# Pooled attention and four experts on one core: first batch in smaller pieces, chunk 0 in another order, batch 1 turned on TensorE

## The chip, the cores and the metric

One core of one Trainium2 chip runs the whole program in one launch. The metric is the device time of an execution in microseconds; the median of five is compared. The profiled execution also has a span, from its first to its last instruction, which is a little shorter.

## The reference

```python
# per batch (8), head (8): 576 queries of 64; keys and values are means of 8 rows
k_p = k.reshape(B, H, 72, 8, 64).mean(axis=3); v_p = ...
attn = softmax(q @ k_p.T / 8);  o = attn @ v_p
x = o.transpose(0, 2, 1, 3).reshape(4608, 512)
p = domain_probs / (domain_probs.sum(-1) + 1e-9)
out = sum over e of p[:, e] * (relu(x @ w1[e]) @ w2[e])   # w1: 512x1024, w2: 1024x512, 4 experts
```

All arrays are float32 in memory. Each expert works on every token, so two thirds and more of the arithmetic are the experts' matrix products.

## The kernel before, in words

**Chunks.** The tokens are worked in nine chunks of 512. Chunk c (0 to 7) holds the first 512 of the 576 queries of batch c; chunk 8 holds the last 64 queries of all eight batches ("remainder", `rem_*`). A chunk's hidden units lie as `H_sb` in four quarters: two halves of F by two halves of tokens.

**Attention of a batch** is a row of pieces, each a Python function that issues its instructions when it is called: the loads (`load_q`, and for keys and values `load_whole` for batches 0 and 1, or `load_part`, four parts that the DMA adds up, from batch 2 on); the pooling (`fold_keys`, `fold_values` on VectorE; for batch 0 `sum_keys`, `sum_values` as matmuls with the identity); `queries` and `keys`, which turn q and the pooled keys so that the head's dimension lies on partitions; `scores` with the exponential on ScalarE; `context`, a product with the pooled values and a column of eights, and a division on VectorE; `turn`, which brings the 128 x 512 token block into `xT`. For batch 0 `turn` uses TensorE with the identity and a copy out of PSUM; for all others a DMA transpose on the SP queue. `queries` and `keys` turn on TensorE for batches 0 and 1 (`BUSY = 2`) and by DMA from batch 2 on. All loads that cast or add go through GpSimd's queue (POOL), in program order with GpSimd's own additions.

**Experts.** In chunk 0, `up` is the plain first layer, one block of 128 hidden units at a time, with the relu on ScalarE; `down` is the second layer of expert 0 in seven products (a scheme of Strassen's kind, with the sums of weights `weight_sums` and of hidden units `hidden_sums` made on VectorE), `down_plain` that of experts 1 and 2. From chunk 1 on both layers are made of seven products instead of eight: `up_product` (with `first_weight_sums`, `x_sum`, and relus on ScalarE and VectorE, `relu_sum`) and `down`. In step 4 of `down` (`POOLED`) the addition to `acc` is GpSimd's, for experts 1 to 3.

**Order.** Everything stands under a manual schedule: the program order is the order of each engine. `attention_first` has batch 0's attention, with `idle(n)`, matmuls on zeros that fill TensorE's time and write nothing used, and then the first layer of expert 0 in token halves. Chunk 0 then runs in four rounds of eight steps, with a table (`pieces_first`) that puts batch 1's attention, weight sums and loads into steps. In the long loop, slot g = 7 t + i issues step i of expert t's first layer for two units and step i - 1 of the `down` of the expert before, thus 2 x 4 + 8 matmuls of 128x128x256. `pieces_later` puts batch b's pieces into slots counted from 28 (b - 2), 28 slots being one chunk:

```python
q_at, k_at, scores_at, contexts_at, loads_at = (
    (4, 10, (14, 15, 16, 17), (18, 19, 20, 22), (12, 14, 13, 16, 19)) if b == 2
    else (-4, -4, (3, 4, 5, 6), (8, 9, 11, 13), (-2, 17, 0, 3, 6)))
```

Here `loads_at` are the slots of the next batch's first part, its q, and its second to fourth part. A `turn` follows its context by one slot. The slot is a place in the program order; GpSimd or SP reach it when what stands before it on their own queue is done.

**Queues at the start.** SP: q of batch 0, in two halves. POOL: k and v of batch 0 in halves, `w1` of experts 0 and 1, the probabilities, `w2` of expert 0, `w1` of expert 2, batch 1's k, q, v, `w1` of expert 3, the other `w2`, the remainder's q, batch 2's first part. A piece `gate` (a small GpSimd copy from batch 1's `xT`) stands ahead of batch 2's second part.

Of the kernel before, what the change touches and what calls it, by code (L numbers as in the profile page):

```python
# [9 lines left out]
ACT = mybir.ActivationFunctionType  # L10
# [7 lines left out]
def kernel(  # L18
# [57 lines left out]
    gate_at = const.tile([1, NR], BF16, name="gate")  # L76
# [27 lines left out]
    def load_whole(b, src, nm):  # L104
# [4 lines left out]
        for hs in groups(b):  # L109
            nc.gpsimd.dma_start(  # L110
                out=raw[:, hs], in_=src[b, hs].rearrange("h (j r) d -> j h r d", r=POOL)
            )
# [10 lines left out]
    def load_q(b):  # L123
        q_sb = raws[("q", b)] = qpool.tile([P, H, NR, D], BF16, name="q_sb")
        src = q[b, :, 0:NT, :].rearrange("h (p r) d -> p h (r d)", r=NR)
        if b:
            nc.gpsimd.dma_start(out=q_sb[:].rearrange("p h r d -> p h (r d)"), in_=src)
            return

        wide = acc[:].rearrange("p r (g t) -> p (r g) t", t=NR * D)  # L130
        for hs in groups(b):
            nc.sync.dma_start(out=wide[:, hs], in_=src[:, hs])
        for pair in range(NPAIR):
# [110 lines left out]
    def sum_keys(hs):  # L244
        kp = sum_pool(raws[("kraw", 0)], hs)
        nc.vector.tensor_copy(out=kp_all[0:SP, hs, 0, :], in_=kp)
        nc.scalar.copy(out=kp_all[0:SP, hs, 1, :], in_=kp)
# [24 lines left out]
    def queries(b, pair=0):  # L272
# [9 lines left out]
        qt_ps = one_bank(b).bitcast(BF16)[:, 0:4 * P].rearrange("p (h a t) -> p h a t", h=2, a=2)  # L282
# [5 lines left out]
        nc.vector.tensor_copy(out=state[("qT", b)][:, 2 * pair:2 * pair + 2], in_=qt_ps)  # L288
# [49 lines left out]
    def turn(b, r):  # L338
# [4 lines left out]
        if b:  # L343
            nc.sync.dma_start_transpose(out=dst, in_=x_tok)
            return
        xt_ps = chains[0][:].bitcast(BF16)[:, 0:KC * P].rearrange("p (k t) -> p k t", t=P)
        for kc in range(KC):
            nc.tensor.transpose(xt_ps[:, kc, :], x_tok[:, kc * P:(kc + 1) * P], ident[:])
        nc.scalar.copy(out=dst, in_=xt_ps)
# [46 lines left out]

    def attention_first():

        lo, hi = groups(0)
        idle(24)  # L400
# [3 lines left out]
        idle(2)  # L404
        keys(0, lo)
        idle(2)
        sum_keys(hi)
        scores(0, 0)
        queries(0, 2)
        queries(0, 3)  # L410
        idle(1)
        scores(0, 1)
        keys(0, hi)
        sum_values(lo)
        scores(0, 2)
        sum_values(hi)
        idle(2)
        scores(0, 3)
        idle(6)
        half = NT // 2  # L420
        context(0, 0)
        context(0, 1)
        idle(3)
        turn(0, 0)
        context(0, 2)
        idle(2)
        turn(0, 1)
        context(0, 3)
        up(0, 0, range(0, 2), slice(0, half))
        turn(0, 2)  # L430
        up(0, 0, range(2, 4), slice(0, half))
        turn(0, 3)
        up(0, 0, range(4, FCH), slice(0, half))
        up(0, 0, range(FCH), slice(half, NT))
# [11 lines left out]
    def up(c, e, fcs, at=slice(0, NT)):  # L446
        xT, H_sb = x_of(c), hidden[(c, e)]
        for fc in fcs:
# [3 lines left out]
            for kc in range(KC):  # L452
# [6 lines left out]
                out=dst, in_=out_ps.rearrange("p (t n) -> p t n", n=HN), func=ACT.Relu)  # L459

# [162 lines left out]
    def down_last(c, e):  # L623
# [3 lines left out]
        for row in (1, 0):  # L627
            for col in range(2):
                cols = slice(col * HD, (col + 1) * HD)
                ps = banks[2 * row + col][:].rearrange("p (j d) -> p j d", j=BLOCKS)  # L630
                for j in range(BLOCKS):
                    for fc in range(FCH):
                        nc.tensor.matmul(  # L633
                            ps[:, j], lhsT=H_sb[:, fc // HF, row, fc % HF, j * P:(j + 1) * P],
                            rhs=last_weights(fc, col), start=(j == 0 and fc == 0),
                            stop=(fc == FCH - 1), skip_group_check=True,
                        )
                for j in range(BLOCKS):
                    add(ps[:, j], c, e, row * BLOCKS + j, cols, False)
# [34 lines left out]
    make_identity(nc, ident[:])  # L674
    every = slice(0, H)

    def gate():

        nc.gpsimd.tensor_copy(out=gate_at[:], in_=state[("xT", 1)][0:1, 0, 0:NT:P])

    def pieces_first():

        at = {}

        def put(s, i, *pieces):
            at.setdefault((s, i), []).extend(pieces)

        def put_each(slots, pieces):
            for slot, piece in zip(slots, pieces, strict=True):
                put(*slot, piece)  # L690

        put(0, 0, *weight_sums(0))
        put_each([(0, i) for i in range(3, 7)], first_weight_sums(0))
# [172 lines left out]
```

## Time and profile before

| | us |
|---|---|
| median of 5 runs (lowest, highest) | 506.93 (506.67, 508.61) |
| profiled execution, its own time | 506.93 |
| its span | 504.8 |
| TensorE busy (weight loads) | 493.8 (407.0) |
| VectorE, ScalarE, GpSimd busy | 377.9, 300.6, 119.4 |
| loaded and stored by DMA queues | 42.48 MB, mean 84 GB/s |

Busy times are sums over the span; TensorE's matmuls are pipelined and their ends are modelled, so what counts there is when the next one starts. In a timeline line the first two numbers are start and duration in us, then engine, line of the kernel, operation and tiles, the number of instructions merged, and in brackets the idle time before and what ended it. GpSimd's DMA instructions (L110 to L171) are issues: the transfer lands later, and the engine's wait before a later issue names the landing.

### The profile page before, as it was taken

The numbers are of one execution on the slowest core, as the hardware profiler recorded it, in microseconds if no ns is written. First come the engines' busy times: TensorE is split into PE (matmuls) and PEld (weight loads), VectorE is DVE, ScalarE is ACT, GpSimd is POOL, SyncE is SP. The second block draws the span as 40 slices with busy tenths as digits, with TensorE's granted clock in tenths as the row PEclk, the third lists the DMA queues.
The fourth block names the chain that finished last, engine by engine and source line by source line (L and its number), as shares of the span: only waits on it lengthen the run. The fifth ranks groups of instructions, "written<-read, shape, count | busy, mean of one in ns | idle before, by whom it ended". The sixth has DMA issues, their size and how long they took to land.

```text
span 504.8 us, 11277 instructions
## 1 busy us (share of the span) xinstructions
PE 493.8 (98%) x4580; PEld 407.0 (81%) x4580; DVE 377.9 (75%) x742; ACT 300.6 (60%) x558; POOL 119.4 (24%) x113
## 2 busy tenths in 40 slices
PE   9999999999999999999999999999999999999995
PEld 4657448878788887988788878888888888888885
DVE  3465689988867887788687868887787767876673
ACT  2675616685576557655766576656755566556650
POOL 6331033462560145112530244010001110111010
PEclk9999999999999999999999999999999999999998
DMA  9999969999699048922793179430310010003003
GB/s 187 209 206 208 201 70 127 151 93 119 67 127 123 8 50 118 126 55 34 66 163 64 26 74 159 47 56 22 84 34 1 22 64 1 12 21 84 1 1 84
DMA packets 106787, 42.48 MB, mean 84 GB/s; under 512 B 79840, under 2 KB 105184, under 8 KB 106736
## 3 DMA queue, kind: packets, MB, share of 16 engines
q0 software_dynamic: 59728, 22.43, 40.7%
q1 hardware_dynamic: 46432, 18.82, 19.3%
q8 instruction: 36, 0.59, 0.5%
q10 hardware_dynamic: 576, 0.52, 0.3%
q14 instruction: 15, 0.12, 0.1%
HBM read 45.69 MB, written 9.44 MB: 109 GB/s over the span
## 4 chain that ended last, share of the span: by engine, by line
PE 90%; DVE 5%; DMA 3%; ACT 1%; issue 1%; DVEq 0%; ACTq 0%
PE o_ps L578 37%; PE unit L510 35%; PE unit L453 5%; DMA xT<-x_tok 3%; PE o_ps L604 3%; PE unit L256 2%; PE att L304 2%; PE unit L633 1%; DVE S L187 1%; DVE acc L649 1%; PE att L330 1%; DVE H L491 1%; PE unit L240 1%; ACT o_ps L586 0%; DVE x_tok L319 0%
## 5 line engine op out<-in xcount | busy, mean ns | idle before, releaser
L649 DVE SCALAR_TENSOR_TENSOR acc<-o_ps,p_all,acc 128x256 f32<-128x256 f32 (+1 forms) x284 | 126.5, 486 | 57.3 <-PE o_ps L578 40.0
L578 PEld LDWEIGHTS <-H 128*128 128x128 bf16 x1320 | 129.1, 98 | 17.7 <-issue 1.6
L510 PEld LDWEIGHTS <-w_bf 128*128 128x128 bf16 x1024 | 98.0, 98 | 18.2 <-issue 6.5
L491 DVE CUSTOM_DVE_ANT_0 H<-unit,partial 128x512 bf16<-128x512 f32 x128 | 87.7, 686 | 23.2 <-PE unit L510 16.9
L578 PE MATMUL o_ps<-w_bf,H 128*128 128x256 bf16 x792 | 102.6, 273 | 0.7 <-ACT o_ps L586 0.6
L510 PE MATMUL unit<-xT,w_bf 128*128 128x256 bf16 x672 | 96.4, 273 | 1.0 <-ACT unit L523 0.7
L592 POOL TENSOR_TENSOR acc<-acc,addend 128x512 f32<-128x512 f32 x24 | 33.1, 1379 | 266.6 <-ACT addend L590 257.8
L525 ACT COPY partial<-unit 128x512 f32<-128x512 f32 x128 | 72.0, 590 | 31.4 <-PE unit L510 30.8
L510 PEld LDWEIGHTS <-wu_bf 128*128 128x128 bf16 x768 | 73.1, 98 | 10.8 <-issue 2.5
L510 PE MATMUL unit<-xs,wu_bf 128*128 128x256 bf16 x512 | 76.9, 273 | 0.0
L578 PE MATMUL o_ps<-wt_bf,H 128*128 128x256 bf16 x528 | 68.4, 273 | 0.0
L578 PEld LDWEIGHTS <-S 128*128 128x128 bf16 x528 | 51.7, 98 | 6.4
L523 ACT COPY unit<-unit 128x512 f32<-128x512 f32 x64 | 37.2, 582 | 31.9 <-PE unit L510 26.1
L527 ACT ACTIVATE H<-unit 128x512 bf16<-128x512 f32 x64 | 38.8, 606 | 27.6 <-PE unit L510 27.6
L531 ACT ACTIVATE H<-unit 128x512 bf16<-128x512 f32 x64 | 38.1, 596 | 27.7 <-PE unit L510 27.5
L510 PE MATMUL unit<-xs,w_bf 128*128 128x256 bf16 x256 | 38.5, 273 | 2.0 <-DVE H L491 2.0
L647 ACT ACTIVATE acc<-o_ps,p_all 128x256 f32<-128x256 f32 x72 | 30.2, 471 | 13.4 <-PE o_ps L578 10.8
L119 POOL DMA_DIRECT2D kraw<-in_k_dram x18 | 25.3, 1405 | 39.0 <-DMA kraw<-in_k_dram 38.8
L578 PE MATMUL o_ps<-w_bf,S 128*128 128x256 bf16 x264 | 34.2, 273 | 0.0
L578 PE MATMUL o_ps<-wt_bf,S 128*128 128x256 bf16 x264 | 34.2, 273 | 0.0
L510 PE MATMUL unit<-xT,wu_bf 128*128 128x256 bf16 x224 | 33.7, 273 | 0.0
L308 ACT ACTIVATE expT<-att 72x1024 bf16<-72x1024 f32 x28 | 28.6, 1020 | 7.8 <-PE att L304 7.8
(112 smaller groups left out, 525.6 us busy)
## 6 DMA issues: line engine op xcount, KB each, us to landing
out_dram<-acc SPq DMA_DIRECT2D x32, 256.0 KB, 3.3
w_bf<-in_moe_w_dram POOLq DMA_DIRECT2D x7, 1024.0 KB, 22.5
q_sb<-in_q_dram POOLq DMA_DIRECT2D x7, 512.0 KB, 10.6
kraw<-in_k_dram POOLq DMA_DIRECT2D x24, 144.0 KB, 5.6
vraw<-in_v_dram POOLq DMA_DIRECT2D x24, 144.0 KB, 6.6
acc<-in_q_dram SPq DMA_DIRECT2D x2, 512.0 KB, 4.6
w_bf<-in_moe_w_dram POOLq DMA_DIRECT2D x2, 512.0 KB, 11.6
wt_bf<-in_k_dram POOLq DMA_DIRECT2D x2, 288.0 KB, 7.7
```

The source lines that it names most:

```text
L119: nc.gpsimd.dma_start(out=raw[:], in_=rows, accum_op=ALU.add)
L308: nc.scalar.activation(out=expT[:, 2 * pair:2 * pair + 2].rearrange("j h a b t -> j b (h a) t"), in_=sc_ps[0:SP].rearrange("j b h (a t) -> ...
L491: nc.vector._custom_dve(TENSOR_ADD_SAT, out=dst, in0=ps, in1=part, s0=LARGEST, s1=0.0)
L510: nc.tensor.matmul(ps[:, n * HN:(n + 1) * HN], lhsT=lhs[:, kc, f:f + P], rhs=rhs[:, kc, :], start=(not grows and n == 0 and kc == 0), stop ...
L523: nc.scalar.copy(out=units[unit][1][:], in_=ps)
L525: nc.scalar.copy(out=part[:, step - 2], in_=ps)
L527: nc.scalar.activation(out=quarter(0, 0), in_=ps, func=ACT.Relu)
L531: nc.scalar.activation(out=quarter(0, 1), in_=ps, func=ACT.Relu)
L578: nc.tensor.matmul(ps[:, j], lhsT=lhs[:, i, j * P:(j + 1) * P], rhs=rhs[:, i, :], start=(not grows and i == 0 and j == 0), stop=(i == HF - 1),
L592: nc.gpsimd.tensor_add(out=dst, in0=dst, in1=addend[:])
L647: nc.scalar.activation(out=dst, in_=o_ps, func=ACT.Copy, scale=prob)
L649: nc.vector.scalar_tensor_tensor(out=dst, in0=o_ps, scalar=prob, in1=dst, op0=ALU.mult, op1=ALU.add,)
```

## The change

1. *Start.* q of batch 0 in halves by two ways: heads 0 to 3 on SP as before, heads 4 to 7 on POOL with the cast in the DMA, behind the two halves of k. The identity is made after the first k load is issued. `w1` of experts 2 and 3 are loaded ahead of batch 1's k, q and v.
2. *Batch 0's attention.* 16 fillers instead of 24 at the start, 20 in all instead of 42. `scores_first` works on four heads and half of the tokens, so that the exponentials of the first 256 tokens are there after two; `sum_keys` splits its copies by heads; the copies of `queries` and `turn` alternate between VectorE and ScalarE. `up_first` does the first layer of expert 0 for 128 tokens at a time (two quarters), two blocks of hidden units to a bank, between contexts and turns; tokens 256 to 511 follow by `up`.
3. *Chunk 0.* `first_chunk` is an order written out: expert 1's first layer; expert 2's with expert 0's `down`; expert 3's with batch 1's queries, keys and scores; then `down_plain` of experts 1 and 2 with batch 1's contexts and turns. Some weight sums go to slots of the long loop.
4. *Batch 1* is turned by TensorE (`turn`: `if b >= BUSY`), with the copy on ScalarE.
5. *Batch 2's loads.* No `gate`; the second and third part and q are issued before chunk 0, the fourth part in slot 3, ahead of GpSimd's first sum. Batches 2 and 3 get other slots.
6. *The end.* In `down_last` the last pair of sums has a bank for each.

```diff
+    def load_q(b, group=None): ...     # group 0: SP and cast copies; group 1 or none: POOL
@@ sum_keys
-        nc.vector.tensor_copy(out=kp_all[0:SP, hs, 0, :], in_=kp)
-        nc.scalar.copy(out=kp_all[0:SP, hs, 1, :], in_=kp)
+        n = (hs.stop - hs.start) // 2
+        for i, copy in enumerate((nc.vector.tensor_copy, nc.scalar.copy)):
+            part = slice(i * n, (i + 1) * n)
+            copy(out=kp_all[0:SP, hs][:, part],
+                 in_=kp[:, part].unsqueeze(2).to_broadcast([SP, n, 2, D]))
@@ turn
-        if b:
+        if b >= BUSY:
             nc.sync.dma_start_transpose(out=dst, in_=x_tok)
             return
@@ attention_first
+        idle(16)
+        sum_keys(lo)
+        queries(0, 0); queries(0, 1)
+        sum_keys(hi)
+        keys(0, lo)
+        queries(0, 2); queries(0, 3)
+        scores_first(0, 0)
+        keys(0, hi)
+        idle(2)
+        scores_first(1, 0); scores_first(0, 1)
+        sum_values(lo)
+        scores_first(1, 1)
+        sum_values(hi)
+        context(0, 0); context(0, 1)
+        idle(2)
+        turn(0, 0)
+        up_first(range(0, 4), first)
+        turn(0, 1)
+        context(0, 2)
+        up_first(range(4, FCH), first)
+        context(0, 3)
+        up_first(range(0, 4), second)
+        turn(0, 2)
+        up_first(range(4, 6), second)
+        turn(0, 3)
+        up_first(range(6, FCH), second)
+        up(0, 0, range(FCH), half)
+    def up_first(fcs, at):
+        for fc in fcs[::2]:
+            out_ps = (units[1] + chains[1:])[turn_of("up", 3)][:, 0:2 * P]
+            for i in range(2):
+                for kc in range(KC):
+                    nc.tensor.matmul(out_ps[:, i * P:(i + 1) * P],
+                        lhsT=w1_bf[:, 0, kc, (fc + i) * P:(fc + i + 1) * P], rhs=xT[:, kc, at], ...)
+            nc.scalar.activation(..., func=ACT.Relu)
@@ pieces_later
-                    (4, 10, (14, 15, 16, 17), (18, 19, 20, 22), (12, 14, 13, 16, 19)) if b == 2
+                    (1, 9, (13, 14, 15, 16), (17, 18, 20, 21), (11, 12, 14, 25, 28)) if b == 2
+                    else (0, 3, (10, 11, 12, 13), (15, 16, 18, 20), (5, 6, 8, 11, 14)) if b == 3
+            if b == 2:
+                put(start + 3, lambda: load_part(2, 3))
+                put(start + 5, lambda: load_q_rem(2))
...
-            for n, slot in enumerate((24, 25, 25, 26) if b == 2 else (16, 16, 20, 23) if b < B
+            for n, slot in enumerate((24, 25, 25, 26) if b == 2 else (24, 24, 25, 26) if b == 3
+                                     else (16, 16, 20, 23) if b < B
@@ the program
+        load_q(0, 0)
+        load_whole(0, k, "kraw", groups(0)[:1])
+        make_identity(nc, ident[:])
+        load_whole(0, k, "kraw", groups(0)[1:])
+        load_q(0, 1)
...
+        load_w1(2)
         load_w2(0)
-        load_w1(2)
+        load_w1(3)
         attention_first()
...
+        load_part(2, 0)
+        load_part(2, 1)
+        load_q(2)
+        load_part(2, 2)
         load_q_rem(0)
         load_q_rem(1)
-        load_part(2, 0)
+        first_chunk()
```

The remainder's pieces of batches 0 and 1 move from slots 0, 5, 9, 10 to 6, 10, 12, 13.

## The prediction

> **What bounds the kernel now.** I read the page's shares and slices first, then the busy time by stage, then the timeline of TensorE for gaps, and last the timelines of GpSimd, SyncE and VectorE around those gaps.
>
> ```profile
> span 504.8 us, 11277 instructions
> PE 493.8 (98%) x4580; PEld 407.0 (81%) x4580; DVE 377.9 (75%) x742; ACT 300.6 (60%) x558; POOL 119.4 (24%) x113
> ...
> DMA  9999969999699048922793179430310010003003
> GB/s 187 209 206 208 201 70 127 151 93 119 67 127 123 8 50 118 126 55 34 66 163 64 26 74 159 47 56 22 84 34 1 22 64 1 12 21 84 1 1 84
> ```
>
> TensorE is busy nearly everywhere, so only three things shorten the run: fewer matmul slots, an earlier start of useful ones, or fewer gaps. The DMA row is saturated for the first five slices (63 us, about 200 GB/s): until then the order of loads decides what is there.
>
> ```profile
> 0.00:22.24 22.24, 20.41 (x154) 11.05 (x155) 9.64 (x28) 8.30 (x11) 11.56 (x20) 1.00 1.08 198
> 22.24:30.32 8.08, 7.61 (x72) 6.71 (x72) 2.79 (x7) 6.80 (x18) 3.99 (x5) 1.00 1.21 207
> 30.32:73.73 43.41, 43.41 (x283) 22.90 (x283) 29.82 (x53) 21.57 (x37) 5.57 (x9) 1.00 1.14 173
> ...
> 124.20:131.20 7.00, 4.88 (x43) 3.92 (x41) 6.81 (x15) 2.38 (x5) 3.27 (x3) 1.00 0.45 83
> ```
>
> Stages (columns: length, then busy PE, PE weight load, DVE, ACT, POOL, clock, DMA share, GB/s): batch 0's attention and filler matmuls last to 22.24; its first layer for expert 0 to 30.32; the rest of chunk 0 to 73.73 without a gap. Then comes the long loop, in slots of 16 matmuls of 128x256 at 109 ns = 1.75 us. At 124 to 131 TensorE lacks 2.1 us, 2.4 with the slower matmuls beside it.
>
> ```profile
> 9.03 0.65 POOL L171 DMA_DIRECT2D p_all<-in_moe_domain_probs_dram  x1 [1.12 <-DMA wt_bf<-in_k_dram]
> 9.19 1.04 PE L240 MATMUL unit<-wt_bf,ident 72*72 72x256 bf16 x8
> 10.06 0.61 PE L285 MATMUL o_ps<-ident,q_sb 128*128 128x128 bf16 x8
> 10.51 0.59 PE L256 MATMUL unit<-H 128*128 128x512 bf16 x2
> ...
> 22.24 0.60 PE L453 MATMUL unit<-xT,w_bf 128*128 128x256 bf16 x4 [0.41 <-ACT xT L349]
> ```
>
> GpSimd's wait tells that the first half of k landed by 9.03; the fillers end at 9.19 and the key sums start. The first layer starts at 22.24, released by the copy of the second turned block.
>
> ```profile
> 115.13 1.40 POOL L119 DMA_DIRECT2D kraw<-in_k_dram  x1 [0.62 <-DMA kraw<-in_k_dram]
> 116.84 1.38 POOL L119 DMA_DIRECT2D vraw<-in_v_dram  x1 [0.31 <-DMA vraw<-in_v_dram]
> ...
> 124.39 0.43 DVE L187 TENSOR_TENSOR xs<-xT 128x512 bf16<-128x512 bf16 x1 [1.72 <-DMA xT<-x_tok]
> ...
> 126.13 0.60 PE L510 MATMUL unit<-xs,w_bf 128*128 128x256 bf16 x4 [0.89 <-DVE H L491]
> ...
> 129.59 0.60 PE L510 MATMUL unit<-xs,w_bf 128*128 128x256 bf16 x4 [1.11 <-DVE H L491]
> ```
>
> The gap's cause: batch 2's last DMA transposes (issued 116.02 and 119.45) share the engines with batch 3's last loads. VectorE, in order, waits 1.72 us for them, then also has batch 3's key and value sums (0.75 and 1.49 us) in hand, and TensorE waits for its relus.
>
> **The change, part by part**
>
> *Start.* Only half of q goes ahead on SP; the first k load goes ahead of the identity's memset on POOL. Both halves of q land by 6.56 (the casts start at 4.78 and 6.56), so the second takes about 1.8 us of a saturated system, and the issue moves from 1.37 to about 0.75. The first half of k then lands between 9.0 - 0.6 - 1.8 = 6.6 and 9.0 - 0.6 = 8.4; I take 7.3. The 16 fillers end near 7.5: the weight loads of before's stand 0.43 apart up to 6.7 us, 0.22 after. So key sums start near 7.5, 1.7 earlier.
>
> Then, by durations of before: key sums 0.87; VectorE and ScalarE copies start 1.07 after the sum and take 0.42 and 0.37. The second half of k lands 1.93 after the first (10.96 - 9.03), 9.2, so its sums run 9.2 to 10.1. The second half of q, now in POOL's queue, lands some 1.3 later (batch 1's whole q took 2.6: 37.2 to 39.8), 10.5. First scores at 11; four exponentials of 1.02 with the q copy ahead of them fill ScalarE to about 16. The second value sum ends at 15.3, and its copy at 15.9. Contexts start at 16.0 (before 18.6), the first division ends at 17.4, its turn's copy at 18.6 (before, context to end of copy: 18.60 to 21.13). The first layer by quarters needs just this one block: it starts at 18.6 instead of 22.24. From there 64 matmuls of 128 columns (3.6), 16 transposes and 2 contexts (1.4) and 32 of 256 columns (3.5) are 8.5. The two last turns share one bank with the copies (0.59, then 0.41), which I count as 0.4 of waits. Expert 1 starts at about 27.4 instead of 30.32: **-2.9** (-3.8 to -1.6).
>
> Here a rule of the Trainium skill speaks against the change: "TensorE: Matmul & The Clock Gate", section "Back-to-back issue gap", gives about 81 ns per matmul where each 128-column matmul has its own weight load. By it the 64 cost 5.2 us, 1.6 more. The row at 10.06 shows eight such pairs in 0.45 us (10.06 to 10.51), 56 ns. I take the row; by the rule the sum would be -1.4.
>
> *Batch 1 turned by TensorE.* Adds 16 transposes in a stage with no free slot and four ScalarE copies of 0.59 (ACT has 21.6 of 43.4 busy there, so those hide). Four transposes take 0.22 (42.66 to 42.88 in TensorE's timeline): **+0.9**. The same page's section on PE-mode transpose gives about 275 ns for one in a kernel: 4.4 us for 16, and a sum of +0.5 in all. Again the row decides, because these are the same shape and neighbours. It takes four DMA transposes (60.1 to 71.0) and GpSimd's gate off their queues; the gate waited 27.04 us for them.
>
> *Chunk 0's order.* The same matmuls. Loads: expert 2's first weights take the place of the second weights of expert 0 (29.4), these land at 34.6, expert 3's first weights at about 39.8, batch 1's k, q, v at 42.4, 45.0, 48.5, and expert 1's second weights at 54.2 as before (all from GpSimd's and VectorE's waits, shifted by 5.2 for one weight load). They are needed at 36.1 (bank opening on TensorE), 47.5, 48 to 55, and 56.6. Slack is 1.5, 8, 3 to 7, 2.4 us, so nothing waits if the loads keep their pace. For bank waits among queries and contexts (each waits for a 0.41 copy or 0.9 division behind it on VectorE, which loses eight weight sums of 0.6 to later slots or other places): **+0.4** (0 to 1.5). The loop starts at about 72.1.
>
> *Batch 2's loads ahead of the sums.* Its second part is no longer held by the gate to 72.0 but by the first part's landing, about 65. Before, from there to the issue of the last part's v is 16.3 us (72.03 to 88.32); so 81.5, and GpSimd's first sum (g = 5, ScalarE's addend ready near 82) comes at 83, a store behind it on SP at 84, the remainder's q transpose at 85, landing 2.4 to 4.4 later; its scores (slot 10) come at 91. **+0.2** (0 to 2).
>
> *Batch 2's attention a slot earlier, batch 3's folds moved from slots 24 and 25 to 31 and 32.* The last transpose is issued 1.75 to 2 us earlier relative to the loop. Batch 3's third part comes after GpSimd's sum of slot 19, thus still beside these transposes (4.4 to 7.7 us each). VectorE's need at 122.7 (before's clock) meets a landing between 121.8 and 125.1, and the folds are out of its way. Of the 2.4 us I take **-2.0** (-2.4 to -0.5).
>
> *New places.* Batch 3's last part follows GpSimd's sum of slot 26: issued 125.3 and 126.7, landing 5 to 6.6 later at 130.3 to 133.3, and its folds come at 131.8 and 133.6: **+0.4** (0 to 4). Batch 3's x sums (four of 0.42) now fall in slots 52 to 54 together with batch 4's folds (0.75 and 0.42 to 1.5): VectorE at about 80% in this stretch gets 3 us more in 5.25, so relus run late: **+0.7** (0 to 2). Its transposes at slots 44 to 49 leave the place at 160, where TensorE loses 0.5: **-0.3** (-0.6 to 0).
>
> *Tail.*
>
> ```profile
> 498.03 0.88 DVE L649 SCALAR_TENSOR_TENSOR acc<-unit,p_all,acc 128x256 f32<-128x256 f32 x2 [0.80 <-PE unit L633]
> ...
> 499.78 0.88 DVE L649 SCALAR_TENSOR_TENSOR acc<-unit,p_all,acc 128x256 f32<-128x256 f32 x2 [0.87 <-PE unit L633]
> ```
>
> The last pair of adds starts when both halves of a bank are done. With its own bank the first add runs beside the last eight matmuls: **-0.4**, with nothing behind it but the store.
>
> *Sum*: -2.9 + 0.9 + 0.4 + 0.2 - 2.0 + 0.4 + 0.7 - 0.3 - 0.4 = **-3.0**. The profiled execution took 506.93, its span 504.8 and 2.1 around it; that is also the median of the five runs. Forecast 503.9.
>
> **The rivals**
>
> *The loads hold it.* The first half of k lands at 8.4 rather than 7.3, with TensorE idle for it, and all after it in the queue likewise; and at slot 24 the transposes are as late as before. Front -1.8, boundary -0.5, no gain at 160: -1.8 + 0.9 + 0.4 + 0.2 - 0.5 + 0.4 + 0.7 - 0.4 = -0.1, 506.8. For it: DMA at 9 tenths in these slices. Against: 512 KB is really taken from ahead of k. Chance 0.16.
>
> *Slower: batch 3's last loads miss their fold.* At slot 31 VectorE, strictly in order, waits for k's last part; behind it stand relus that free TensorE's banks, and the 1.72 us wait before cost 2.4. With lateness d the loss is d + 0.7, in place of my 0.4: 503.5 + d + 0.7. The gain is gone at d = 2.7, and it is slower by 0.3% from d = 4.3; at 5 it is 509.2. It needs the sum of slot 26 to be held on GpSimd, as it was by 8.82 us for VectorE at 127.04. Against: that hold came of the gap which goes. Chance 0.14.
>
> *More than forecast.* The boundary's wait goes wholly, slot 52 costs nothing, the front gives 3.6: 0.4 + 0.7 + 0.7 more, 502.1. Chance 0.12. The main case has 0.58.
>
> **How the numbers follow.** 0.3% is 1.5 us, about what a measurement here can tell from none: faster is under 505.4, slower over 508.45. Main case and the better one lie under 505.4 together: 0.70. Same 0.16, slower 0.14. The likeliest cases alone span 501 to 505.5; to hold 8 in 10 the range takes in the first rival and half-late loads: 500.9 to 508.0.
>
> **What would show it.** Right: key sums near 7.5, first layer near 18.6 and at 56 ns per 128-column matmul, expert 1 near 27.4, the loop's start near 72, no VectorE wait for xT at slot 24, a last add of 0.49 alone. Wrong: key sums at 8.4 or later with TensorE idle ahead; the bank opening waiting for w2; scores of the remainder waiting for qTr; VectorE waiting for kraw or vraw at slots 31 and 32; gaps at slot 52 or after.

## The result, and the profile after

The changed kernel took 503.52 us (median of 40 runs), the kernel before 507.67 us (77 runs beside them): a ratio of 0.9914, 95% interval 0.9898 to 0.9931. By the ratio that is 4.4 us less (by the two medians 4.2), where 3.0 were forecast and 503.9 us were named. That the median lies so close to 503.9 is partly luck: the kernel before took 507.67 us here, not the 506.93 from which the forecast was counted. The ratios leave out disturbed executions, the medians do not.

The profiled execution took 502.04 us. Its page answers to the one of before:

```profile
span 500.3 us, 11351 instructions
PE 490.2 (98%) x4622; PEld 407.1 (81%) x4622; DVE 372.9 (75%) x741; ACT 302.4 (60%) x561; POOL 119.5 (24%) x113
...
DMA  9999999989499759923894179740210010004003
GB/s 161 212 210 203 203 84 129 131 66 100 59 136 66 91 68 123 106 54 38 75 160 57 29 77 149 45 64 22 86 33 1 22 64 1 12 23 85 1 0 85
```

The work of the engines is nearly the same, VectorE's 5 us less. So the gain lies in starts and gaps. The stages, cut where the same matmuls stand (columns as in the prediction):

```profile
0.00:18.33 18.33, 14.96 (x129) 9.04 (x130) 7.03 (x21) 8.05 (x11) 11.32 (x20) 1.00 1.07 176
18.33:27.52 9.19, 8.74 (x124) 7.97 (x124) 4.60 (x11) 6.13 (x16) 3.94 (x5) 1.00 1.13 214
27.52:71.99 44.47, 44.38 (x298) 23.71 (x298) 28.64 (x50) 24.46 (x42) 7.93 (x8) 1.00 1.15 174
...
123.05:130.05 7.00, 6.46 (x59) 5.49 (x57) 6.96 (x15) 3.38 (x7) 4.26 (x3) 1.00 0.34 54
```

The first layer starts 3.9 us earlier and takes 1.1 more; the rest of chunk 0 takes 1.06 more (44.47 for 43.41); in the 7 us that begin 3.92 us after slot 24 starts, TensorE is busy for 6.46, before 4.88.

Where the 4.9 us between the two profiled executions (506.93 and 502.04) come from:

| stretch | before | after | difference | forecast |
|---|---|---|---|---|
| start to the loop (slot 0) | 73.73 | 71.99 | -1.74 | -1.6 |
| slots 0 to 56 | 108.67 | 106.81 | -1.86 | -1.0 |
| slot 56 to the last first-layer product | 309.20 | 308.81 | -0.39 | 0 |
| from there to the end of the span | 13.22 | 12.65 | -0.57 | -0.4 |
| around the span | 2.1 | 1.8 | -0.3 | 0 |

The timeline of the front:

```profile
1.34 0.91 POOL L109 DMA_DIRECT2D wt_bf<-in_k_dram  x1 [0.89 <-POOLq L914]
...
7.49 1.04 PE L242 MATMUL unit<-wt_bf,ident 72*72 72x256 bf16 x8
...
18.33 0.61 PE L494 MATMUL unit<-xT,w_bf 128*128 128x128 bf16 x8 [0.67 <-ACT xT L357]
...
19.70 1.06 PE L494 MATMUL unit<-xT,w_bf 128*128 128x128 bf16 x16
20.59 0.42 PE L337 MATMUL att<-vp,expT 72*128 72x65 bf16 x8
...
22.86 0.39 PE L355 MATMUL o_ps<-ident,x_tok 128*128 128x128 bf16 x4 [0.28 <-ACT xT L357]
```

The key sums start at 7.49 (forecast 7.5), the first layer at 18.33 (18.6). Sixteen products of 128 columns go from 19.70 to 20.59, 56 ns each, as the row of before had said and not the 81 ns of the rule. The wait at 22.86 (0.28 us) is one of those for the shared bank, which were forecast as 0.4.

The timeline of slots 21 to 28:

```profile
113.57 1.38 POOL L118 DMA_DIRECT2D kraw<-in_k_dram  x1
114.43 1.94 POOL L118 DMA_DIRECT2D vraw<-in_v_dram  x1
...
123.09 0.43 DVE L189 TENSOR_TENSOR xs<-xT 128x512 bf16<-128x512 bf16 x1 [1.57 <-DMA xT<-x_tok]
...
126.08 0.90 DVE L189 TENSOR_TENSOR xs<-xT,xs 128x512 bf16<-128x512 bf16 x1
...
128.29 1.03 PE L552 MATMUL unit<-xT,w_bf 128*128 128x256 bf16 x8 [0.47 <-ACT unit L565]
```

VectorE still waits 1.57 us for the turned block (1.72 before), against the forecast; yet TensorE loses only 0.87 us here, before 2.61. I count a loss from start to start, against 109 ns for a product of 256 columns, gaps over 0.2 us only, and use this number for all kernels below.

The tail:

```profile
494.03 1.36 DVE L695 SCALAR_TENSOR_TENSOR acc<-unit,p_all,acc 128x256 f32<-128x256 f32 x3 [0.80 <-PE unit L678]
...
495.78 0.48 DVE L695 SCALAR_TENSOR_TENSOR acc<-o_ps,p_all,acc 128x256 f32<-128x256 f32 x1 [0.39 <-PE o_ps L678]
```

One addition stands alone at the end, where two did.

### The profile page after: what moved, and what is told of

It is laid out like the page before. It is cut to its first block, busy times and chain, and to the rows that moved or that the text cites. A ratio compares the mean times of both kernels' runs of the same rounds, so it can differ in the third digit from the quotient of the medians.

```text
span 500.3 us, 11351 instructions
## 1 busy us (share of the span) xinstructions
PE 490.2 (98%) x4622; PEld 407.1 (81%) x4622; DVE 372.9 (75%) x741; ACT 302.4 (60%) x561; POOL 119.5 (24%) x113
## 4 chain that ended last, share of the span: by engine, by line
PE 86%; DVE 7%; DMA 2%; ACT 2%; issue 1%; POOL 1%; DVEq 0%; ACTq 0%; POOLq 0%
PE o_ps L620 37%; PE unit L552 36%; PE unit L479 5%; DVE acc L695 2%; PE o_ps L646 2%; DMA wt_bf<-in_v_dram 2%; PE att L311 1%; PE att L337 1%; PE unit L678 1%; DVE H L533 1%; DVE S L189 1%; DVE x_tok L326 1%; DVE xs L189 1%; DVE wt_bf L189 0%; ACT o_ps L628 0%
## 5 line engine op out<-in xcount | busy, mean ns | idle before, releaser
L315 ACT ACTIVATE expT<-att 72x1024 bf16<-72x1024 f32 x26 | 26.5, 1020 | 7.1 <-PE att L311 7.1
```

The source lines that it names most:

```text
L315: nc.scalar.activation(out=expT[:, 2 * pair:2 * pair + 2].rearrange("j h a b t -> j b (h a) t"), in_=sc_ps[0:SP].rearrange("j b h (a t) -> ...
```

## The experiments

The theory going in: the front gains by earlier loads and smaller pieces and keeps its gain to the end; the gap at slots 24 to 28 closes because batch 2's attention runs earlier. The rivals: the gain of the front is the loads' alone, the gap is cured by something else than the new slots, and GpSimd's sums decide by chance. Both kernels and the twelve experiments stand in one table; "expert 1", "slot 0" and "end" are the times in us at which TensorE starts its first layer, starts the loop, and the span ends; "loss" is TensorE's around slots 24 to 28. All but the ratio come from one profiled execution of each kernel. The front is the same in the changed kernel, e3, e4, e8 and e12, and there expert 1 starts between 27.30 and 28.04 us; differences within such a width are not effects.

| kernel | expert 1 | slot 0 | loss | end | ratio to before (95%) |
|---|---|---|---|---|---|
| before | 30.32 | 73.73 | 2.61 | 504.8 | 1 |
| changed | 27.52 | 71.99 | 0.87 | 500.3 | 0.9914 (0.9898, 0.9931) |
| e1 front of before | 29.22 | 73.69 | 1.53 | 504.6 | 0.9975 (0.9949, 1.0001) |
| e2 token halves | 29.08 | 73.55 | 1.80 | 504.3 | 0.9963 (0.9924, 1.0001) |
| e3 batch 1 by DMA | 28.04 | 71.35 | 0.60 | 506.9 | 1.0042 (1.0015, 1.0069) |
| e4 slots of before | 27.40 | 71.87 | 0.97 | 499.9 | 0.9915 (0.9887, 0.9942) |
| e5 late loads | 32.52 | 76.99 | 0.60 | 512.2 | 1.0052 (1.0021, 1.0083) |
| e6 halves, filled | 27.73 | 72.20 | 1.63 | 502.1 | 0.9921 (0.9891, 0.9952) |
| e7 q ahead | 28.65 | 73.12 | 0.60 | 501.9 | 0.9948 (0.9913, 0.9983) |
| e8 sums later | 27.30 | 71.78 | 0 | 499.3 | 0.9882 (0.9851, 0.9912) |
| e9 filled | 28.12 | 72.60 | 1.55 | 501.3 | 0.9889 (0.9849, 0.9929) |
| e10 late loads, filled | 27.70 | 72.17 | 2.40 | 502.8 | 0.9967 (0.9930, 1.0004) |
| e11 later and filled | 27.88 | 72.35 | 0 | 499.0 | 0.9896 (0.9862, 0.9931) |
| e12 no GpSimd sum | 27.86 | 72.33 | 0 | 501.2 | 0.9942 (0.9910, 0.9973) |

### e1: the front of before in the changed kernel

```diff
-        idle(16)
+        idle(24)
...
         load_q(0, 0)
-        load_whole(0, k, "kraw", groups(0)[:1])
+        load_q(0, 1)
         make_identity(nc, ident[:])
-        load_whole(0, k, "kraw", groups(0)[1:])
-        load_q(0, 1)
+        load_whole(0, k, "kraw")
...
```

Both halves of q go on SP, and `attention_first`, its copies and its token halves are those of before.

> The changed kernel with batch 0's front as it was before (both halves of q on SP, the identity made ahead of k, 42 fillers, whole scores, the first layer in token halves); all from expert 1 on stays changed. Theory, that a start won at the front is kept to the end: expert 1 starts near 30 us instead of 27.5, the long loop near 74.6 instead of 72.0, the span is 2.5 to 3 us over the changed kernel's 500.3. Rival, that the load stream or batch 1's chain sets the loop's start: the loop starts at 72 to 73 all the same and the span is within 0.7 us of 500.3.

Measured: 0.9975, slot 0 at 73.69, 1.70 us behind the changed kernel and level with before. Chunk 0 took the same 44.47. So the front is worth 1.7 us at the loop, and the rest of the 4.3 us between the two spans is lost later: 0.66 us more at slots 24 to 28, and near 252, 266 and 306 us gaps of 0.92, 1.03 and 0.94 us that the changed kernel has smaller or not at all, in instructions that are the same. What moved is only their phase against GpSimd and the loads (see e12). At slots 24 to 28 the trace shows the meeting:

```profile
126.91 1.50 DVE L190 TENSOR_TENSOR xT<-xT 128x512 bf16<-128x512 bf16 x1
...
126.87 1.26 POOL L633 TENSOR_TENSOR acc<-acc,addend 128x512 f32<-128x512 f32 x1 [8.79 <-ACT addend L631]
```

An addition of 0.42 us takes 1.50 beside GpSimd's sum, the relu's last step on VectorE stands behind it, and TensorE waits for that. The same 1.50 stands in e2, e6 and e9, and these four lose 1.53 to 1.80 us here; in the changed kernel and e7 GpSimd's sum meets the next addition instead (0.90 and 1.03 us), and the loss is 0.87 and 0.60. In these six the code of this stretch is the same, so the changed kernel's 0.87 is a good draw and not a fixed size.

### e2 and e6: token halves instead of quarters

```diff
         turn(0, 0)
-        up_first(range(0, 4), first)
-        turn(0, 1)
         context(0, 2)
-        up_first(range(4, FCH), first)
+        turn(0, 1)
         context(0, 3)
-        up_first(range(0, 4), second)
+        up(0, 0, range(0, 2), slice(0, HN))
...
```

> The changed kernel with expert 0's first layer in token halves (256 columns, two turned blocks needed) instead of quarters; loads and scores stay changed. Theory, that quarters are worth what they start earlier and cost 56 ns each: first layer at about 20 us instead of 18.3, expert 1 about 0.6 to 1 us later, span 0.5 to 1 us longer. Rival, that the turns and divisions of the last blocks end the stage either way: expert 1 within 0.2 us, span unchanged.

Measured: expert 1 at 29.08, 1.56 us later; it looks as if quarters were worth all of that. But the busy time by stage of e2 shows the clock (the column before the last two) at a half:

```profile
16.00:19.00 3.00, 2.63 (x28) 1.81 (x28) 2.04 (x7) 0.59 (x1) 0.75 (x1) 0.52 1.20 213
19.00:22.00 3.00, 2.86 (x23) 2.22 (x23) 1.87 (x4) 0.41 (x2) 0.85 (x1) 0.50 1.13 216
```

The first layer ran at 213 ns for a product of 256 columns in these 6 us. So the run could not tell. e6 repeats it with ten fillers where TensorE waits:

```diff
         keys(0, lo)
+        idle(2)
         queries(0, 2)
...
         scores_first(0, 0)
+        idle(2)
...
+        idle(2)
         sum_values(hi)
         context(0, 0)
+        idle(2)
         context(0, 1)
...
         turn(0, 0)
+        idle(2)
         context(0, 2)
```

> Token halves in the first layer, as in the earlier run with halves (expert 1 at 29.08 us instead of 27.52, but its granted clock was 0.5 from 16 to 22 us), with ten filler matmuls more where TensorE waits between 9 and 18 us, to keep the clock up. Nothing else differs. Theory 1 (quarters gain because the first layer can start with one turned block): clock 1.00 throughout, first layer at 20.0 us, expert 1 at 28.5, some 1 us behind the changed kernel, loop start 73.0. Theory 2 (most of the earlier loss was the clock): expert 1 within 0.3 us of the changed kernel, 27.5 to 27.8, and a ratio near 0.9915. Bounds: if the fillers themselves get in the way, expert 1 is later than 29.1.

```profile
16.00:19.00 3.00, 2.74 (x36) 1.72 (x36) 2.12 (x6) 0.59 (x1) 0.75 (x1) 1.00 1.19 212
19.00:22.00 3.00, 2.27 (x30) 2.00 (x28) 1.83 (x4) 1.23 (x4) 0.85 (x1) 1.00 1.13 216
```

Measured: the clock at 1.00, the first layer at 20.09 as expected, and expert 1 at 27.73, only 0.21 us behind the quarters. The rival holds. Quarters start 1.76 us earlier (18.33), but then take 9.19 us, with two turns and two contexts and three bank waits among them, where halves take 7.64. Quarters with eleven fillers (e9, e10, e11) start expert 1 at 28.12, 27.70 and 27.88, so that at a full clock no gain of quarters over halves is seen at all.

### e3: batch 1 turned by DMA transposes

```diff
-        if b >= BUSY:
+        if b:
             nc.sync.dma_start_transpose(out=dst, in_=x_tok)
```

> The changed kernel with batch 1 turned by DMA transposes again, 16 TensorE transposes fewer; order and loads stay changed. Theory, that the TensorE turns pay: 0.9 us of TensorE is saved, but four transposes beside the weight loads and batch 2's added loads land at 73 us or later, VectorE's x sums wait for them in order, and TensorE loses more than it saved: span 0.5 to 3 us longer. Rival, that they land in time: loop's start 0.9 us earlier, span 0.9 us shorter.

```profile
78.77 0.43 DVE L189 TENSOR_TENSOR xs<-xT 128x512 bf16<-128x512 bf16 x1 [5.47 <-DMA xT<-x_tok]
...
79.70 1.01 PE L552 MATMUL unit<-xs,wu_bf 128*128 128x256 bf16 x4 [4.28 <-DVE xs L189]
```

Measured: from expert 1 to slot 0 it takes 43.31 us instead of 44.47, so that turning batch 1 costs TensorE 1.16 us (forecast 0.9); slot 0 itself comes only 0.64 earlier, because expert 1 started later in this execution. Then VectorE waits 5.47 us for the last block and TensorE 4.28 for VectorE; the end is 6.6 us later. That is beyond what I expected of it. Part of it is the clock, which stands at 0.53 from 78 to 80 us and at 0.50 from 80 to 84, after TensorE's pause. In the changed order batch 1's contexts stand at the end of chunk 0, and a DMA transpose has no time to land: the last was issued at 70.07 and landed at 78.67. The turn on TensorE is what makes this order possible, not a price beside it.

### e4: the slots of batches 2 and 3 as before

```diff
-                    (1, 9, (13, 14, 15, 16), (17, 18, 20, 21), (11, 12, 14, 25, 28)) if b == 2
-                    else (0, 3, (10, 11, 12, 13), (15, 16, 18, 20), (5, 6, 8, 11, 14)) if b == 3
+                    (4, 10, (14, 15, 16, 17), (18, 19, 20, 22), (12, 14, 13, 16, 19)) if b == 2
...
-            for n, slot in enumerate((24, 25, 25, 26) if b == 2 else (24, 24, 25, 26) if b == 3
+            for n, slot in enumerate((24, 25, 25, 26) if b == 2
                                      else (16, 16, 20, 23) if b < B
```

> The changed kernel with the slots of batches 2 and 3 of before (attention, loads of batches 3 and 4, x sums); batch 2's loads stay early, the fourth part in slot 3. Theory, that the slots cure the gap after slot 24: the gap comes back with 1 to 2.5 us and the one at slot 49 with 0.5, span 1.5 to 2.5 us longer. Rival, that batch 2's early loads cure it: span within 0.5 us.

Measured: 0.9915, and a loss of 0.97 us. Beside the early loads the new slots show no gain: the six kernels that have both lose 0.60 to 1.80 (e1). With the early loads kept, the last turned block landed 8.50 us after slot 21 started (before 9.52, changed 9.37), VectorE waited 0.69 us for it, and the value fold took 0.42 us instead of 1.49; in the kernel before GpSimd's sum had started 0.41 us ahead of that fold (127.04 and 127.45) and held it. The new slots without the early loads were not tried.

### e5 and e10: batch 2's loads late again

```diff
         turn(1, 3)
+        nc.gpsimd.tensor_copy(out=gate_at[:], in_=state[("xT", 1)][0:1, 0, 0:NT:P])
+        load_part(2, 1)
+        load_q(2)
+        load_part(2, 2)
+        load_part(2, 3)
+        load_q_rem(2)
...
-        load_part(2, 0)
-        load_part(2, 1)
-        load_q(2)
-        load_part(2, 2)
         load_q_rem(0)
         load_q_rem(1)
+        load_part(2, 0)
```

Both stand on top of e4, with its slots of before.

> The changed kernel with the slots of batches 2 and 3 of before, as in the run with those slots alone (ratio 0.9915, gaps of 0.97 us at slots 24 to 28), and now also with batch 2's later loads held as before: a copy on GpSimd that reads batch 1's turned blocks, then part 1, q, part 2, part 3 and the remainder's q, all ahead of the loop; part 0 again goes behind the remainders of batches 0 and 1. Theory 1 (the early loads of batch 2 cured TensorE's gap at slots 24 to 28, because its attention no longer runs late against batch 3's loads): the gap returns to about 2.4 us, VectorE waits over 1.5 us for the turned block, and the ratio is about 0.995. Theory 2 (GpSimd's sum near slot 31 and a VectorE addition meet by chance, and only the new phase of the two separates them): the gap stays near 1 us where the sum does not meet the value fold, ratio about 0.992, and comes back only if the value fold is stretched to about 1.5 us again.

This run decided nothing, for two reasons. The clock was at 0.50 from 13 to 25 us and the loop began 5 us late; and my edit had left the remainder's transpose on SP behind batch 2's q, so that TensorE stood 4.80 us near 96 for its scores. Its loss of 0.60 later on says nothing, since that stand had given the loads their time. e10 mends both: remainder in its slots of before, and the fillers of e9.

> The late loads of batch 2 once more, without the flaw of the earlier run with late loads (there the remainder's q transpose stood on SP behind batch 2's q and held its scores 4.8 us): remainder in its slots of before (0, 5, 9, 10), slots of batches 2 and 3 and x sums of before, the copy on GpSimd that waits for batch 1's turned blocks ahead of batch 2's later parts; and the 11 fillers, to keep the clock up. So it is the loop of before behind the changed front. Theory 1 (batch 2's early loads cured the gap at slots 24 to 28): VectorE waits over 1.5 us for the turned block, TensorE loses about 2.4 us at slots 24 to 28, ratio 0.993 to 0.995. Theory 2 (a chance meeting of GpSimd's sum with the value fold decided): TensorE loses 1 us or less there unless a fold is stretched, ratio near 0.990.

```profile
71.08 0.18 POOL L789 COPY gate<-xT 1x4 bf16<-1x4 bf16 x1 [24.40 <-ACT xT L358]
...
124.78 0.43 DVE L190 TENSOR_TENSOR xs<-xT 128x512 bf16<-128x512 bf16 x1 [2.10 <-DMA xT<-x_tok]
125.12 0.75 DVE L224 TENSOR_TENSOR kp<-kraw 72x512 bf16<-72x512 bf16 x2
...
126.53 0.60 PE L557 MATMUL unit<-xs,w_bf 128*128 128x256 bf16 x4 [1.27 <-DVE H L538]
```

Measured: GpSimd waits 24.40 us in its copy as it did before, and the gap is back: VectorE waits 2.10 us, the folds stand right behind it, and TensorE loses 2.40 us, with the value fold at its plain 0.42. So a stretched value fold is not needed for the gap; against e4 (0.97) the late loads cost 1.43 us here, against e9 (1.55), which has the same front, 0.85. Another 1.57 us went near 95, where VectorE has weight sums in slots of the changed kernel and an addition of 2.47 us beside GpSimd's sum; neither the kernel before nor the changed one loses there.

### e7: the loads of the front alone undone

```diff
         load_q(0, 0)
-        load_whole(0, k, "kraw", groups(0)[:1])
-        make_identity(nc, ident[:])
-        load_whole(0, k, "kraw", groups(0)[1:])
         load_q(0, 1)
+        make_identity(nc, ident[:])
+        load_whole(0, k, "kraw")
```

Both halves of q are on SP again.

> The changed kernel with both halves of batch 0's q on SP ahead and the identity's memset ahead of k on GpSimd, as before; the order of the pieces (quarters) stays changed. It tells what the loads alone are worth in the front. Theory 1 (k's landing sets the front): key sums near 8.5 us, expert 1 later by 0.8 to 1.2 us, at about 28.5, loop start about 73.0, ratio 0.9935. Theory 2 (the pieces' order carries the front, and the values' sums, which come last, set its end): expert 1 within 0.4 us of the changed kernel, ratio 0.9915 to 0.992.

```profile
4.58 2.90 PE L262 MATMUL unit<-H 128*128 128x512 bf16 x8
8.74 1.03 PE L243 MATMUL unit<-wt_bf,ident 72*72 72x256 bf16 x8 [1.26 <-DMA wt_bf<-in_k_dram]
```

Measured: the fillers end and TensorE waits 1.26 us for k; key sums at 8.74 for 7.49, expert 1 at 28.65, 1.13 later, slot 0 also 1.13 later. By these profiles the loads are worth 1.1 of the front's 1.7 us and the order of its pieces the other 0.6 (e1). The first lies outside the width of 27.30 to 28.04 by 0.61 us; the second is no larger than that width and is not shown.

### e8: the sums of turned blocks two slots later

```diff
-            for n, slot in enumerate((24, 25, 25, 26) if b == 2 else (24, 24, 25, 26) if b == 3
+            for n, slot in enumerate((26, 27, 27, 28) if b in (2, 3)
                                      else (16, 16, 20, 23) if b < B
```

> The changed kernel with the sums of turned blocks on VectorE of batches 2 and 3 two slots later (slots 26, 27, 27, 28 of each batch instead of 24, 25, 25, 26), so that VectorE no longer waits in order for the last turned block with relus behind it. Theory 1 (the wait of 1.57 us for the turned block at slot 24 makes TensorE's gaps of 0.24 and 0.63 us there, and likewise 0.59 at slots 52 to 56): no wait for the turned block, these gaps go, the end is 0.8 to 1.5 us earlier, ratio about 0.989. Rival (VectorE has no room left in these slots, and the sums only move the gaps to slots 28 to 31, or into GpSimd's sum): no change, ratio 0.9905 to 0.993.

```profile
123.15 0.69 DVE L533 CUSTOM_DVE_ANT_0 H<-unit,partial 128x512 bf16<-128x512 f32 x1
123.76 0.42 DVE L189 TENSOR_TENSOR xs<-xT 128x512 bf16<-128x512 bf16 x1
...
127.21 1.04 PE L552 MATMUL unit<-xT,w_bf 128*128 128x256 bf16 x8
128.09 1.04 PE L620 MATMUL o_ps<-w_bf,H 128*128 128x256 bf16 x8
```

Measured: VectorE does not wait for the block any more, and the losses at slots 24 to 28 and 52 to 56 are gone. Slots 21 to 56 take 64.25 us, for 65.17 in the changed kernel and 67.62 before. The ratio of 0.9882 and the median of 501.48 us are better than the changed kernel's; the intervals of the two ratios overlap a little, so that it is the trace that shows the 0.9 us. The loss is 0 in the other two kernels with this edit too (e11, e12).

### e9 and e11: fillers for the clock

```diff
         keys(0, lo)
+        idle(2)
         queries(0, 2)
...
         scores_first(0, 0)
+        idle(2)
...
         context(0, 0)
+        idle(2)
         context(0, 1)
-        idle(2)
+        idle(4)
         turn(0, 0)
+        idle(3)
```

> The changed kernel with 11 filler matmuls more in its front, where TensorE waits anyway: 2 ahead of the third block of queries, 2 after the first scores, 2 between the first two contexts, 2 more ahead of the first turn and 3 after it. Nothing else differs. Theory 1 (executions of the changed kernel that take 505 to 509 us are those in which the granted clock falls to about a half somewhere in the front's waits, as it did with halves): the runs draw together at 501 to 503 us at a mean clock of 0.998 or more, and the ratio falls from 0.9914 to about 0.989. Theory 2 (the low clock comes from outside the kernel): the spread stays, with a third of the runs over 505 us, ratio 0.991. If the fillers get in the way, the first layer starts over 0.3 us later than at 18.33.

Measured: eight runs from 501.42 to 504.12 us, with a mean granted clock of 0.998 or more in each. Of 41 executions of the changed kernel, the profiled one included, eleven had a mean clock of 0.989 or less and took 506.4 to 509.9 us; the 23 at 0.998 or more took 500.5 to 504.7. Over all kernels with such fillers (e6, e9, e10, e11) none of 36 executions was under 0.995; the like kernels without them had 4 of 12 (e7), 2 of 12 (e2, e12), 1 of 9 (e4), none of 6 (e8) at 0.989 or less, and e1, whose front has the 42 fillers of before, none of 12. That speaks for theory 1: the low clock starts in the front's waits. The bound was passed too: the first layer started at 18.93, 0.6 us later (18.51 and 18.69 in e10 and e11), so that the fillers take back some of what they save.

> The sums of turned blocks two slots later (ratio 0.9882 alone) together with the 11 fillers. Theory (the two gains are independent): runs within 500.5 to 502.5 us, ratio 0.986 to 0.988. Rival (the runs with later sums had a full clock anyway, and the fillers add nothing or cost 0.2 us): 0.988 to 0.989.

Measured: 0.9896, median 501.12 us, span 499.0. Seven of ten runs lie in the expected 500.5 to 502.5. The two gains are not independent as far as these runs can tell: the ratio is no better than that of either edit alone (0.9882 in e8, 0.9889 in e9), although e11 has the lowest median of all.

### e12: GpSimd sums nothing

```diff
-        POOLED = (4,)
+        POOLED = ()
```

on top of e8.

> The sums of turned blocks two slots later, and GpSimd takes none of the output sums (24 additions of 128x512 go back to VectorE as 48 of 0.43 us). Theory 1 (a VectorE addition of two bf16 operands is held while GpSimd adds: 2.5 us instead of 0.69 where they meet, and TensorE's gaps of about 0.8 us near 250 and 0.35 near 302 come of that): no addition on VectorE over 0.95 us, these gaps vanish. What it costs: VectorE gains some 21 us of work and the stretch of about 5.5 us goes; if it has room, the end is 0.5 to 1.5 us earlier than with GpSimd's sums (span 499.3). Rival (VectorE at 75 to 80% has no room in the slots with attention): new gaps at slots 10 to 60, the end 1 to 4 us later.

What it is about, in the timeline of before:

```profile
249.68 2.72 DVE L187 TENSOR_TENSOR S<-H 128x1024 bf16<-128x1024 bf16 x1
...
250.01 1.83 POOL L592 TENSOR_TENSOR acc<-acc,addend 128x512 f32<-128x512 f32 x1
```

An addition of 0.69 us takes 2.72 while GpSimd adds. Measured in e12: no VectorE addition of two operands in SBUF is stretched, TensorE's gaps near 250 and 302 are gone, and from slot 56 to the end it takes 320.18 us, the least of all kernels here (e8 321.65, changed 321.46). But it ends 1.9 us later than e8: it is 0.55 behind at slot 0, another 0.79 at slot 21 (three gaps of 0.28 to 0.41 between 86 and 91 us) and another 1.99 at slot 56, of which one gap near slot 39 makes 2.03, and 1.47 come back after slot 56. These lines of e12's timeline show that gap:

```profile
148.56 0.84 ACT L693 ACTIVATE acc<-o_ps,p_all 128x256 f32<-128x256 f32 x2 [2.10 <-PE o_ps L620]
149.29 1.01 ACT L315 ACTIVATE expT<-att 72x1024 bf16<-72x1024 f32 x1
...
150.35 0.39 PE L311 MATMUL att<-qT,kpT 64*128 64x256 bf16 x4 [1.86 <-ACT expT L315]
```

The exponential stands on ScalarE behind two writes to `acc`, and the next scores wait for the exponential. The product named in the bracket is not what held the writes: theirs had ended at 146.32. The chain of waits shows what did:

```profile
140.27 8.21 DMA out_dram<-acc
148.48 0.02 issue
148.50 0.02 ACTq L693
148.52 0.05 issue
148.56 0.12 ACT acc L693
```

ScalarE's queue waits for the store of the chunk before, which reads the rows of `acc` that are to be overwritten. It took 8.21 us. In e8 the same store was issued at 139.02 and had landed by 143.98, and ScalarE did not wait. A likely reason, not tried: without the sum that GpSimd's queue waited for, the next batch's q was issued at 138.50 and so ahead of the store; in e8 it followed at 140.15.

So theory 1 is right on the stretched additions. The rival's forecast came in place and size (gaps between slots 10 and 60, 1 to 4 us), but the large gap is not want of room on VectorE, which stood idle for 2.02 us at 147.32; the three small ones were not followed up. A kernel with GpSimd's sums up to slot 56 and without them after was not tried.

## Why the prediction was right, and where its steps were not

*The direction and the size.* Faster, by 4.4 us for 3.0: inside the range. The profiled executions differ by 4.9 us, 1.9 more than the sum: 0.4 after slot 56 and 0.3 around the span were in no term, slots 0 to 56 gave 0.9 more than forecast, and front and tail 0.3 more.

*Start, -2.9: measured -2.80, but its parts were not those of the working.* "The issue moves from 1.37 to about 0.75" failed: k's first load is still issued at 1.34. The landing (8.74 before, 6.70 now, forecast 7.3 from bounds of 6.6 and 8.4) came from q's half that no longer goes ahead. That the key sums start at 7.49, as forecast, is in part luck: they wait for the fillers, which stand 0.43 us apart up to a moment that differs from execution to execution (4.58 to 7.14 us in the fourteen profiles, 7.06 here) and 0.22 after it; with the same front they start at 6.88 in e4 and at 7.61 in e8. The loads are worth 1.1 us (e7); the 0.6 for the order of pieces (e1 against e7) is within the spread, and quarters over halves show no gain (e6). The last 1.1 us of the difference between the two profiles at expert 1 is also there in e1, which has the front of before: 0.67 of it already at the key sums (8.52 for 9.19), with the same loads ahead. That part is the fillers' pace: in the kernel before it doubles at 7.03 us and the fillers end 0.45 us after k has landed, in e1 it doubles at 5.01 and k's landing (8.48) decides. The rest is a wait of 0.47 us for ScalarE just ahead of expert 1, which e1 does not have. A forecast of a front from one profile has that much play.

*Batch 1 on TensorE and the chunk's order, +0.9 and +0.4: measured +1.06 together* (44.47 for 43.41). Without the transposes the stage takes 43.31 (e3), so that they cost 1.16 and the order nothing (-0.10). What the step left out is the other side: without them the changed order would lose 6.6 us (e3).

*Batch 2's loads ahead, +0.2:* the last part's v was issued at 79.34 (81.5), the q transpose of the remainder landed at 90.81, and TensorE lost 0.24 us near 88.9. Right in itself; but the step did not see that these loads also close most of the boundary gap (e4, e10).

*Boundary, -2.0 and +0.4: measured -1.74, for another reason.* The failed step is "the last transpose is issued 1.75 to 2 us earlier relative to the loop": it was issued 4.07 us after slot 21 for 4.67, and landed 9.37 for 9.52, still beside batch 3's third part. With blocks as late as before, what is left is that batch 3's folds no longer stand behind the wait on VectorE; no run has that move alone. What the runs do show: with the slots of before and late loads the loss is 2.4 to 2.6 (before, e10), with the early loads it is 0.97 (e4) and with early loads and new slots 0.60 to 1.80, by the addition that GpSimd's sum happens to hold (e1), and with sums that come after the landing it is 0 (e8, e11, e12). The working had also taken the 1.49 us for the fold's own length, which is 0.42. The folds' new place cost nothing: the last part landed at 132.04 and 133.53, and the folds came at 134.66 and 136.71.

*Slot 52, +0.7: measured +0.59, for another reason.* Not 3 us more of work but one x sum, which takes 1.16 us for 0.42 beside GpSimd's sum (178.23 and 177.85), delays the relu behind it; so this size is luck. *The gap at 160, -0.3: measured -0.66. Tail, -0.4: measured -0.57.*

*The rivals.* "The loads hold it" fell with k's landing at 6.70. "Slower" fell with the folds, though the argument against it was wrong: GpSimd still waits 8.81 us ahead of its sum of slot 26. "More than forecast" came closest in what was gained (4.8 us), though not by its own reasons: slot 52 was not free, the boundary did not close wholly, and the front gave 2.80.

## What to carry to other kernels

When an engine that works in order waits for a transfer, ask first what stands behind the wait: moving the waiting instruction itself by two slots took the whole loss away here (e8), where the earlier transfer left 0.97 us and, with the work behind the wait moved too, 0.60 to 1.80. Before a smaller tile is credited with a gain, run the larger one at the same clock: here the half-rate clock made next to nothing look like 1.6 us. When a trace names a product that had ended long before, look for a transfer that the same wait includes (e12). And a slower engine that takes work over, like GpSimd here, can hold the engine that it relieves; look for one operation with two durations in the trace.

## What the runs showed of the hardware

- VectorE additions with both operands in SBUF are held while GpSimd adds: `S<-H` took 2.72 us for 0.69 beside a GpSimd addition of 1.83, itself 1.27 in the median. All VectorE additions of that kind that meet GpSimd's took 8.4 us over the median of their shape before, 4.5 after and nothing in e12; the 37 multiply-and-adds with one operand in PSUM that met it before stayed at 0.49 or less. The Trainium skill, "SBUF — State Buffer", section "Who interferes with whom", says that a VectorE instruction with two SBUF inputs contends with a GpSimd instruction that reads SBUF, and that the order of issue decides which one is blocked. In e1 that fits: the addition recorded 0.04 us after GpSimd's took 1.50 for 0.42, and GpSimd's its plain 1.26. At 249.68 it does not: the VectorE addition, recorded as first by 0.33 us, was held for 2 us, and GpSimd's for 0.6.
- The granted clock can fall to a half without a long pause of TensorE: in e2 no pause between 8 and 16 us was over 0.4 us, with TensorE busy 1.60 of 2, 2.44 of 3 and 2.38 of 3 us, and from 16 to 22 us the clock was 0.5. The same skill, "TensorE: Matmul & The Clock Gate", section "A second HAM failure mode: psum-queue depth-cycling", tells of such micro-pauses; with ten or eleven fillers more the mean clock was 0.995 or more in all 36 executions here. A long pause lowered it as well: after 4.28 us in e3 it was 0.50 from 80 to 84 us.
- Every changed kernel has about 1.8 us around its span where before had 2.1. Why, no run here shows.
